# Value products of a key group issued one slot later, in front of that slot's transposes: pooled attention followed by two expert layers

## The chip, the cores and the metric

The kernel runs on one core of a Trainium2 chip. The metric is the device time of one execution in microseconds (us); three runs of the kernel before took 1357.13, 1360.44 and 1360.38 us, a median of 1360.38 us.

## The reference

The input is 4 batches of 8 heads, 1152 tokens, head dimension 64, in float32. Queries are pooled in pairs (the mean of two neighbours), so each head has 576 query rows against 1152 keys:

```
q_pool = q.reshape(B, H, S // 2, 2, D).mean(axis=3)
scores = scale * q_pool @ k.T;  scores -= max
attn = exp(scores) / (sum + 1e-9)
x = attn @ v                      # 4 x 576 rows of 512 columns after joining the heads
h = x @ w_in;  g = max(0.01 * h, h);  x1 = g @ w_out              # 512 -> 2048 -> 512
y = max(x1 @ w1, x1 @ w2, x1 @ w3);  out = y @ w2_out             # 512 -> 768 -> 512
```

## The kernel before

**Attention.** Two heads make a pair: 4 pairs a batch, 16 in all. A pair has two phases, ph 0 (320 query columns a head) and ph 1 (256), and a phase has nine slots, one for each tile of 128 keys. In slot s the program writes the four transposes of p for that key tile (`probs_t`, tile pst, copied by ScalarE, ACT, at line 377 into the buffer pt). Three slots make a key group. In the third slot of a group in ph 0 it also writes three transposes of the "mixed" query tile, one for each key tile of the group (`probs_m`, tile psf, copied by VectorE, DVE, at line 384 into columns 256 to 319 of all three parts of pt). The value products (`values`, tile pv) of a group are six matmuls in the program and twelve records in the trace, from pt and v.

Each slot also carries what `now(s)` has scheduled for it: scores of the next phase (six matmuls into three banks s, or twelve for the mixed tile; DVE takes the maximum at line 334, ACT the exponential at line 335), and the transposes that prepare q and k of the next pair (psq, psk). The same three banks s are used by every score tile from pair 4 on, so a score tile's first matmul waits for the exponential of the tile before.

**Experts.** The experts of a batch run beside the attention of the batch after it. After its own work a slot yields its cost and the caller then issues expert products, in portions that a ratio of costs (RATIO, AHEAD) and a target for each slot (CHAIN less what the slot has issued) set. They are the m products of 512 columns (tile f is the f-th of 16 tiles of the first hidden layer: ACT line 730, DVE line 731 writes the high part of g, GpSimd, POOL, line 732 the remainder), then three products each for y (remainder by POOL, line 670), then the o products of 256 columns. Every operand is split into a high part and a remainder, and a product takes three matmuls for each 128 of depth, the third of which needs the remainder. The event `batch` (after the last value products of a batch) issues what is left of the experts and starts the next; `room` does the same in part.

**What sets the order.** Each engine has one instruction stream. The program order is a priority; a scheduler with a model of durations then fixes the order of every engine, so a change of the program also moves instructions that it does not name. PE (TensorE), DVE, ACT, POOL and the DMA queue of SyncE (SP) then take their own stream in order. Lines 105 to 119 keep the value products of a group together. Line 205 (POOL) adds the two rows of each pair of queries of the next q as soon as the load of line 171 has landed, and that load waits for PE's transposes of the q before it, since there is one buffer. During the experts of batch 0 weights are also decoded: ACT line 589, DVE lines 592 and 595, ACT line 610 and POOL line 611. PSUM: three banks s, one pv, and four banks in rotation for everything else.

Of the kernel before, what the change touches and what calls it, by code (L numbers as in the profile page):

```python
# [22 lines left out]
def kernel(  # L23
# [97 lines left out]
    def transpose(out, in_, eye):  # L121
        return on_pe(nc.tensor.transpose, out, in_, eye)
# [7 lines left out]
    def bank(name):  # L130
        turn[0] += 1
        pool = ps_w["m"] if ps_w and turn[0] % 2 == 0 else ps_m
        return pool.tile([128, 512], F32, tag="m", name=name)
# [30 lines left out]
    def load_pair(n):  # L164
        b, hp = divmod(n, NP)
        h0 = 2 * hp
        qr = raw_p.tile([QP, 2, QC, 2, D], F32, tag="q", name="qraw")
        kr = raw_p.tile([128, 2, KT, D], F32, tag="k", name="kraw")

        def load_q(j0, j1):  # L170
            nc.sync.dma_start(
                out=qr[:, j0:j1].rearrange("p h c r d -> p h (c r) d"),
                in_=q[b, h0 + j0:h0 + j1].rearrange("h (p c) d -> p h c d", p=QP),
            )

        def load_k(j0, j1):
            nc.sync.dma_start(out=kr[:, j0:j1], in_=k[b, h0 + j0:h0 + j1].rearrange("h (p c) d -> p h c d", p=128))

        for j0, j1 in ((0, 1), (1, 2)) if n == 0 else ((0, 2),):
            load_q(j0, j1)  # L180
            load_k(j0, j1)
        raws[n] = [qr, kr]
# [4 lines left out]
    def load_v(n):  # L187
        b, hp = divmod(n, NP)
        h0 = 2 * hp
        if n == 2:  # L190
            t = acc_p.tile([128, KDM, TM], F32, tag="acc", name="vacc").rearrange("p m t -> p (m t)")
            vss[n] = t[:, 0:2 * KT * D].rearrange("p (h c d) -> p h c d", h=2, c=KT)
        elif n == 3:
            t = x_p.tile([128, 2, T], F32R, tag="x", name="vx").bitcast(F32).rearrange("p a t -> p (a t)")
            vss[n] = t.rearrange("p (h c d) -> p h c d", h=2, c=KT)
        else:
            vss[n] = vs_p.tile([128, 2, KT, D], F32, tag="v", name="v")
        nc.sync.dma_start(out=vss[n], in_=v[b, h0:h0 + 2].rearrange("h (p c) d -> p h c d", p=128))

    def pool_q(n, j0=0, j1=2):  # L200
        qr = raws[n][0][:, j0:j1]
        for e in range(2):
            engine = nc.vector if n == 0 and j0 == 0 else nc.gpsimd
            a = [qr[:, :, e::2, r] for r in range(2)]
            engine.tensor_tensor(out=a[1 - e], in0=a[0], in1=a[1], op=ALU.add)

    def prep_k(n, j):
        kr = raws[n][1][:, j].rearrange("p c d -> p (c d)")
        ps = bank("psk")
        for i in range(4):  # L210
            transpose(ps[:, i * 128:(i + 1) * 128], kr[:, i * 128:(i + 1) * 128], ident)
        split_k(n, j, [(slice(e * 512, (e + 1) * 512), ps[64 * e:64 * e + 64, 0:512]) for e in range(2)])
# [75 lines left out]
    def keys_of(p, kt):  # L288
        c, k0 = divmod(kt * 128, SN)
        if c == 2:  # L290
            return p[1][:, k0:k0 + 128]
        return p[0].rearrange("p a b -> p (a b)")[:, kt * 128:(kt + 1) * 128]
# [47 lines left out]
    def normalise(n, ph, i):  # L340
        rs = sums[n, ph]
        c = slice(i, i + 1)
        if n < FREE:
            if i < len(tiles_of(ph)) - 1:
                return
            c = slice(0, i + 1)
        if n < NP:
            nc.vector.tensor_tensor(out=rs[:, c], in0=rs[:, c], in1=rs[:, 8:9 + i], op=ALU.add)
        nc.vector.tensor_scalar(out=rs[:, c], in0=rs[:, c], scalar1=1e-9, scalar2=None, op0=ALU.add)
        nc.vector.reciprocal(out=rs[:, c], in_=rs[:, c])  # L350
        if n >= FREE or i == 4:
            p = ptl[n, ph, i]
            for x in p[2:] or p:
                nc.vector.tensor_scalar(out=x, in0=x, scalar1=rs[:, i:i + 1], scalar2=None, op0=ALU.mult)  # L354
# [13 lines left out]
    def probs_t(n, ph, kt):  # L368
        g = kt % PG
        if g == 0:  # L370
            pts[kt // PG] = pt_p.tile([128, PG, 2 * X0], F32, tag="pt", name="pt")
        w = (X0, T - X0)[ph]
        ps = bank("pst")
        for i in range(4):
            transpose(ps[:, i * 128:(i + 1) * 128], keys_of(ptl[n, ph, i], kt), ident)
        dst = pts[kt // PG][:, g, 0:2 * w].rearrange("p (j c) -> p j c", j=2)[:, :, 0:256]
        nc.scalar.copy(out=dst, in_=ps.rearrange("p (j c) -> p j c", j=2))  # L377
# [65 lines left out]
    def attention():  # L443
        npair = B * NP
        load_pair(0)
        for j in range(2):
            pool_q(0, j, j + 1)
            prep_q(0, j)
            prep_k(0, j)
            if j == 0:  # L450
                for i in range(2):
                    scores(0, 0, i)
                    normalise(0, 0, i)
        load_v(0)
        load_pair(1)
        for n in range(1, NP):
            load_v(n)
        spare_tiles()
        for i in range(2, 5):
            scores(0, 0, i)  # L460
            normalise(0, 0, i)
        phases = [(n, ph) for n in range(npair) for ph in range(2)]
        todo = {}

        def at(slot, cost, f, *args):
            todo.setdefault(slot, []).append((f, args, cost))

        def now(slot):
            spent = 0
            for f, args, cost in todo.pop(slot, []):  # L470
                f(*args)
                spent += cost
            return spent

        for u, (n, ph) in enumerate(phases):
            s0 = u * KT
            if u + 1 < len(phases):
                nxt = phases[u + 1]
                k = len(tiles_of(nxt[1]))
                for i in range(k):  # L480
                    if nxt[0] < NP:
                        t = max(0, s0 + KT - EARLIER - 2 * (k - 1 - i))
                    else:
                        t = s0 + S_AT[nxt[1]][i]
                    at(t, QK * 6 * (1 + (i == 4)), scores, *nxt, i)
                    at(t + 1, 0, normalise, *nxt, i)
            if ph == 0 and n + 1 < npair:
                early = n + 1 < NP
                when = PREP_AT[0 if early else 1]
                at(max(0, s0 + (-8 if early else 1)), 0, pool_q, n + 1)  # L490
                for j in range(2):
                    at(max(0, s0 + when[2 * j]), TR * 3, prep_q, n + 1, j)
                    at(max(0, s0 + when[2 * j + 1]), TR * 4, prep_k, n + 1, j)
                if n + 2 < npair:
                    at(max(0, s0 + (-2 if early else 15)), 0, load_pair, n + 2)
                if n + 1 >= NP:
                    at(s0 + 8, 0, load_v, n + 1)
            if n < FREE:
                at(s0 + 4, TR * 2, spread, n, ph)
        if wide:  # L500
            for c in range(PRE):
                at(6 + c * (2 * NP * KT - 8) // PRE, 0, predecode, c)

        late = []

        def follow():
            pn, pph, pgr = late.pop()
            values(pn, pph, pgr)
            if pgr == KT // PG - 1:
                last = pn % NP == NP - 1  # L510
                if pph == 0 and last:
                    yield "room"
                evac(pn, pph)
                if pph == 1 and last:
                    yield "batch"
            return PG * 4 * (X0, T - X0)[pph] / 2400 + 0.565

        for s in range(len(phases) * KT):
            n, ph = phases[s // KT]
            gr, g = divmod(s % KT, PG)  # L520
            done = 0
            want = CHAIN
            if s == 2 * NP * KT:
                done += yield from follow()
            probs_t(n, ph, gr * PG + g)
            done += TR * 4
            if g == PG - 1 and ph == 0:
                probs_m(n, gr)
                done += TR * PG
                want -= TR * PG  # L530
            c = now(s)
            if g == 0 and late:
                c += yield from follow()
            done += c
            yield done, max(0, want - c)
            yield 0, None
            if g == PG - 1:
                late.append((n, ph, gr))
        yield from follow()
        assert not todo  # L540
# [324 lines left out]
```

## Time and profile before

| | us |
|---|---|
| three runs, median | 1360.38 |
| the profiled execution | 1356.42 |
| its span | 1354.7 |
| PE busy in the span | 1259.0 (93%) |
| PE weight loads | 1015.6 (75%) |
| DVE, ACT busy | 627.9, 633.5 |
| POOL busy | 292.1 |

The span has five stages. Attention of batch 0 runs alone until about 215 us. Stage A (215 to 533 us) is attention of batch 1 beside the experts of batch 0, stage B (533 to 828) and stage C (828 to 1119) the same for the batches after it, and from 1119 us the experts of batch 3 run alone. In the timeline a row's two numbers are its start and the length up to the end of the last instruction merged into it; matmul ends are modelled and overlap the next start, so the time that a row took on PE is read from start to start.

### The profile page before, as it was taken

What the parts mean: (1) busy time and instruction counts of PE and PEld (TensorE: products, weight loads), DVE (VectorE), ACT (ScalarE), POOL (GpSimd) and SP (SyncE); (2) the same over time, 40 slices, a digit from 0 to 9 for tenths busy, and PEclk for the clock granted to TensorE, in tenths of its full rate; (3) what the DMA queues carried; (4) which work ended last, traced back from release to release, by engine and by line L of the source; (5) the groups of instructions that cost most, each with busy time, mean ns of one, the idle gap of its engine ahead of it and who ended that gap; (6) DMA issues with size and microseconds to landing.
All of it is one profiled execution on the core that took longest, in us unless ns stands there. A gap on an engine that the chain in (4) does not pass through costs nothing.

```text
span 1354.7 us, 19162 instructions
## 1 busy us (share of the span) xinstructions
PE 1259.0 (93%) x7376; PEld 1015.6 (75%) x7376; DVE 627.9 (46%) x1106; ACT 633.5 (47%) x1253; POOL 292.1 (22%) x265
## 2 busy tenths in 40 slices
PE   5788878899898989999999989999999999999998
PEld 4556646677676877777787878787877788888888
DVE  5655554556656563455555454545464401222110
ACT  5767665666566664544444344545454422112111
POOL 1111022344454330121121010111110002224110
PEclk8888989999999999999999999999999999999999
DMA  5422053666767663444435344535343244333333
GB/s 158 123 74 57 18 149 118 215 210 209 248 202 229 208 188 131 132 136 131 154 126 157 123 128 163 149 109 150 128 141 116 95 154 154 129 126 124 108 126 109
DMA packets 86902, 193.29 MB, mean 143 GB/s; under 512 B 11292, under 2 KB 41756, under 8 KB 86812
## 3 DMA queue, kind: packets, MB, share of 16 engines
q1 hardware_dynamic: 86812, 192.08, 45.1%
q8 instruction: 58, 0.95, 0.3%
q14 instruction: 32, 0.26, 0.1%
HBM read 146.80 MB, written 35.13 MB: 134 GB/s over the span
## 4 chain that ended last, share of the span: by engine, by line
PE 75%; DMA 9%; DVE 7%; ACT 4%; issue 3%; POOL 2%; DVEq 0%; SPq 0%; ACTq 0%; POOLq 0%
PE m L108 41%; PE pv L108 10%; PE s L108 10%; PE pst L108 6%; PE o L108 6%; DMA wraw<-in_moe_w_out_dram 3%; DMA wraw<-in_moe_w_in_dram 2%; DMA wraw<-in_moe_w_dram 2%; DMA qraw<-in_q_dram 2%; DVE mx L334 1%; DVE wmant L595 1%; DVE mx L324 1%; ACT pt L377 1%; DVE q L259 1%; POOL wsplit L611 1%
## 5 line engine op out<-in xcount | busy, mean ns | idle before, releaser
L108 PE MATMUL m<-x,w 128*128 128x512 f32 x1224 | 308.9, 397 | 0.0
L108 PEld LDWEIGHTS m<-x,w 128*128 128x128 f32 x1224 | 222.7, 188 | 54.0 <-issue 12.8
L377 ACT COPY pt<-pst 128x512 f32<-128x512 f32 x288 | 167.4, 587 | 183.5 <-PE pst L108 182.3
L108 PE MATMUL s<-kt,q 128*128 128x384 f32 x840 | 190.6, 358 | 26.8 <-ACT p L335 14.1
L334 DVE TENSOR_REDUCE mx<-s 128x1 f32<-128x1152 f32 x108 | 146.4, 1355 | 116.2 <-PE s L108 114.9
L108 PEld LDWEIGHTS s<-kt,q 128*128 128x128 f32 x840 | 148.2, 195 | 39.2 <-ACT p L335 16.8
L108 PE MATMUL pst<-ident,p 128*128 128x128 f32 x1080 | 169.4, 277 | 8.4 <-ACT pt L377 3.5
L335 ACT ACTIVATE p<-s,mx 128x1152 f32<-128x1152 f32 x108 | 132.4, 1226 | 83.0 <-DVE mx L334 82.3
L108 PEld LDWEIGHTS pst<-ident,p 128*128 128x128 f32 x1080 | 131.6, 141 | 45.1 <-issue 11.6
L732 POOL TENSOR_TENSOR g<-t,g 128x512 fp32r<-128x512 f32 x64 | 84.5, 1322 | 369.7 <-DVE g L731 355.1
L108 PE MATMUL pv<-pt,v 128*64 128x320 f32 (+1 forms) x1008 | 149.9, 435 | 14.0 <-DVE pt L384 13.4
L108 PE MATMUL m<-g,w 128*128 128x512 f32 x576 | 149.8, 399 | 0.0
L108 PEld LDWEIGHTS m<-g,w 128*128 128x128 f32 x576 | 103.6, 188 | 24.5 <-issue 6.2
L108 PEld LDWEIGHTS pv<-pt,v 128*64 128x64 f32 x1008 | 67.8, 143 | 70.0 <-issue 20.5
L108 PE MATMUL m<-x,wsplit 128*128 128x512 f32 x408 | 108.5, 405 | 1.0 <-DVE kt L223 0.8
L730 ACT ACTIVATE t<-m 128x512 f32<-128x512 f32 x80 | 44.3, 555 | 128.2 <-PE m L108 128.2
L611 POOL TENSOR_TENSOR wsplit<-wmant,wsplit 128x512 fp32r<-128x512 f32 x56 | 74.1, 1327 | 92.8 <-ACT wsplit L610 71.0
L108 PEld LDWEIGHTS m<-x,wsplit 128*128 128x128 f32 x408 | 74.7, 191 | 20.5 <-issue 5.1
L731 DVE CAST g<-t 128x512 fp32r<-128x512 f32 x64 | 28.7, 448 | 111.2 <-ACT t L730 110.7
L760 DVE TENSOR_TENSOR t<-m,t 128x512 f32<-128x512 f32 (+1 forms) x60 | 38.2, 637 | 84.9 <-PE m L108 73.8
L670 POOL TENSOR_TENSOR y<-t,y 128x512 fp32r<-128x512 f32 x24 | 31.7, 1319 | 199.1 <-ACT y L669 199.1
L354 DVE TENSOR_SCALAR p<-p,sums 128x1152 f32<-128x1152 f32 x76 | 66.2, 870 | 2.7
(106 smaller groups left out, 1467.7 us busy)
## 6 DMA issues: line engine op xcount, KB each, us to landing
w<-w SPq DMA_DIRECT2D x168, 512.0 KB, 3.5
w<-wsplit SPq DMA_DIRECT2D x56, 512.0 KB, 5.1
wraw<-in_moe_w_out_dram SPq DMA_DIRECT2D x22, 512.0 KB, 4.1
wraw<-in_moe_w_dram SPq DMA_DIRECT2D x18, 512.0 KB, 4.0
qraw<-in_q_dram SPq DMA_DIRECT2D x15, 576.0 KB
kraw<-in_k_dram SPq DMA_DIRECT2D x15, 576.0 KB, 6.9
q<-q SPq DMA_DIRECT2D x52, 160.0 KB, 4.5
wraw<-in_moe_w_in_dram SPq DMA_DIRECT2D x16, 512.0 KB, 5.7
```

The source lines that it names most:

```text
L108: mm = f(*args, **kwargs)
L259: nc.vector.scalar_tensor_tensor(out=lo, in0=src, scalar=scale, in1=hi, op0=ALU.mult, op1=ALU.subtract)
L334: nc.vector.tensor_reduce(out=mx[:, 0:1], in_=ps[:, :, 0:SN], axis=AX.XY, op=ALU.max, negate=True)
L335: nc.scalar.activation(out=p[2], in_=ps[:, :, 0:SN], func=ACTF.Exp, bias=mx[:, 0:1], accum_out=rs[:, i:i + 1])
L354: nc.vector.tensor_scalar(out=x, in0=x, scalar1=rs[:, i:i + 1], scalar2=None, op0=ALU.mult)
L377: nc.scalar.copy(out=dst, in_=ps.rearrange("p (j c) -> p j c", j=2))
L611: nc.gpsimd.tensor_tensor(out=t[:, 1], in0=r, in1=t[:, 0], op=ALU.subtract)
L670: nc.gpsimd.tensor_tensor(out=t[:, 1], in0=src, in1=t[:, 0], op=ALU.subtract)
L730: nc.scalar.activation(out=t, in_=ps[:, 0:k.n], func=ACTF.Prelu, alpha=0.01)
L731: nc.vector.tensor_copy(out=gt[:, 0], in_=t)
L732: nc.gpsimd.tensor_tensor(out=gt[:, 1], in0=t, in1=gt[:, 0], op=ALU.subtract)
L760: nc.vector.tensor_tensor(out=t, in0=ps[:, 0:k.n], in1=t, op=ALU.max)
```

## The change

Before, the value products of a finished group are written in the first slot of the next group (g == 0), behind that slot's transposes and scheduled work, and then the slot's expert products follow. After, they are written at the start of the second slot (g == 1), in front of its transposes: one portion of expert products, that of the first slot, now stands between. The evacuation of pv and the events `room` and `batch`, which follow the last group of a phase, move with them. The value products' cost now counts in the second slot's portion. The last group of all, and the last group of batch 0, are written where they were.

```
             if s == 2 * NP * KT:
                 done += yield from follow()
+            c = 0
+            if g == 1 and late:
+                c += yield from follow()
             probs_t(n, ph, gr * PG + g)
             done += TR * 4
             if g == PG - 1 and ph == 0:
                 probs_m(n, gr)
...
-            c = now(s)
-            if g == 0 and late:
-                c += yield from follow()
+            c += now(s)
             done += c
```

On PE, at the first key group of pair 8 (start of stage B), before; m are expert products, x the attention output, w the weights:

```order
L108 MATMUL m<-x,w 128x512 x3
L108 MATMUL pst<-ident,p 128x128 x8
L108 MATMUL psf<-ident,p 128x128 x3
L108 MATMUL pv<-pt,v 64x320 x6
L108 MATMUL m<-x,w 128x512 x15
```

And the same group after the change:

```order
L108 MATMUL pst<-ident,p 128x128 x4
L108 MATMUL psf<-ident,p 128x128 x3
L108 MATMUL s<-kt_4345,q_123 128x384
L108 MATMUL s<-kt_4345,q_124 128x384
L108 MATMUL s<-kt_4345,q_123 128x384
L108 MATMUL s<-kt_4345,q_124 128x384
L108 MATMUL s<-kt_4345,q_123 128x384
L108 MATMUL s<-kt_4345,q_124 128x384
L108 MATMUL m<-x,w 128x512 x17
L108 MATMUL pst<-ident,p 128x128 x4
L108 MATMUL m<-x,w 128x512 x7
L108 MATMUL pv<-pt,v 64x320 x6
```

The value products stood directly behind psf; now a tile of scores, 24 m products and four transposes stand between.

On POOL, from the first g of stage B to its last, before (g are the remainders of the 16 expert tiles, qraw the pooling of the next q in two halves):

```order
L732 TENSOR_TENSOR g<-t,g 128x512 x4
L205 TENSOR_TENSOR qraw<-qraw 72x8x64 x2
L732 TENSOR_TENSOR g<-t,g 128x512 x8
L205 TENSOR_TENSOR qraw<-qraw 72x8x64 x2
L732 TENSOR_TENSOR g<-t,g 128x512 x4
```

And after (line numbers below the change are one higher):

```order
L733 TENSOR_TENSOR g<-t,g 128x512 x4
L205 TENSOR_TENSOR qraw<-qraw 72x8x64 x2
L733 TENSOR_TENSOR g<-t,g 128x512 x7
L205 TENSOR_TENSOR qraw<-qraw 72x8x64
L733 TENSOR_TENSOR g<-t,g 128x512
L205 TENSOR_TENSOR qraw<-qraw 72x8x64
L733 TENSOR_TENSOR g<-t,g 128x512 x4
```

The first half of the second qraw has moved in front of the twelfth g, that of tile 11.

On POOL at the end of stage A, before (wsplit is a weight's remainder, mb a copy of row sums, x the attention output):

```order
L611 TENSOR_TENSOR wsplit<-wmant,wsplit 128x512
L360 COPY mb<-sums 128x256
L611 TENSOR_TENSOR wsplit<-wmant,wsplit 128x512 x2
L670 TENSOR_TENSOR y<-t,y 128x512
L205 TENSOR_TENSOR qraw<-qraw 72x8x64 x2
```

And after:

```order
L612 TENSOR_TENSOR wsplit<-wmant,wsplit 128x512 x2
L360 COPY mb<-sums 128x256
L205 TENSOR_TENSOR qraw<-qraw 72x8x64 x2
L612 TENSOR_TENSOR wsplit<-wmant,wsplit 128x512
L671 TENSOR_TENSOR y<-t,y 128x512
```

The last y of batch 0's experts has moved from in front of qraw to behind it and one wsplit.

## Rows read from the trace of the kernel before

**Rows 1.** Busy time by stage: stretch, length, each engine, PEclk, DMA share, GB/s.

```profile
215.00:533.00 318.00, 294.74 (x1687) 233.76 (x1686) 180.00 (x281) 191.05 (x360) 123.93 (x102) 0.98 0.62 201
533.00:828.00 295.00, 284.97 (x1651) 228.29 (x1650) 148.76 (x260) 134.37 (x251) 45.77 (x35) 0.99 0.44 136
828.00:1119.00 291.00, 284.90 (x1675) 228.93 (x1674) 132.88 (x231) 126.25 (x235) 38.99 (x30) 1.00 0.43 135
```

**Rows 2.** Waits of PE, whole span then stage A: total us, times, longest.

```profile
PE pv L108 <- DVE pt L384: 13.4, 15, 3.5
...
PE pv L108 <- DVE pt L384: 6.8, 4, 3.5
PE s L108 <- ACT p L335: 6.6, 5, 4.0
```

**Rows 3.** Timeline of PE, stage A: start, us, what, [idle before, releaser].

```profile
232.25 1.84 PE L108 MATMUL pv<-pt,v 128*64 128x320 f32 x12 [2.33 <-DVE pt L384]
...
369.20 2.29 PE L108 MATMUL s<-kt,q 128*128 128x384 f32 x6 [4.02 <-ACT p L335]
...
478.76 1.83 PE L108 MATMUL pv<-pt,v 128*64 128x320 f32 x12 [3.50 <-DVE pt L384]
```

**Rows 4.** Timeline of PE, stages B and C, four places.

```profile
579.66 0.66 PE L108 MATMUL pst<-ident,p 128*128 128x128 f32 x4 [0.71 <-DVE pt L384]
...
789.77 0.28 PE L108 MATMUL psq<-ident,kraw 128*64 128x128 f32 x1
...
801.20 0.57 PE L108 MATMUL o<-w,y 128*128 128x256 f32 x1 [3.70 <-POOL y L670]
...
834.09 1.31 PE L108 MATMUL s<-kt,q 128*128 128x384 f32 x6 [1.45 <-ACT p L335]
```

**Rows 5.** Busy time and PEclk behind two waits, columns as in rows 1.

```profile
478.70:481.00 2.30, 2.23 (x14) 1.20 (x15) 0.44 (x2) 1.45 (x3) 0.00 (x0) 1.00 0.34 127
...
801.20:804.90 3.70, 3.70 (x13) 1.50 (x13) 0.00 (x0) 0.37 (x1) 0.00 (x0) 0.54 0.14 40
```

**Rows 6.** Timeline of SP and POOL in stage B: loads of q and their pooling.

```profile
572.72 0.33 SPq L171 DMA_DIRECT2D qraw<-in_q_dram  x1
...
580.63 2.52 POOL L205 TENSOR_TENSOR qraw<-qraw 72x512 f32<-72x512 f32 x2 [17.59 <-DMA qraw<-in_q_dram]
...
645.68 0.33 SPq L171 DMA_DIRECT2D qraw<-in_q_dram  x1
...
652.11 2.50 POOL L205 TENSOR_TENSOR qraw<-qraw 72x512 f32<-72x512 f32 x2 [6.28 <-DMA qraw<-in_q_dram]
...
717.72 0.33 SPq L171 DMA_DIRECT2D qraw<-in_q_dram  x1
...
723.21 2.50 POOL L205 TENSOR_TENSOR qraw<-qraw 72x512 f32<-72x512 f32 x2 [1.09 <-PE pst L108]
...
799.38 1.77 POOL L670 TENSOR_TENSOR y<-t,y 128x512 fp32r<-128x512 f32 x1
```

**Rows 7.** The page's costliest groups: busy, mean ns of one, idle before.

```profile
L611 POOL TENSOR_TENSOR wsplit<-wmant,wsplit 128x512 fp32r<-128x512 f32 x56 | 74.1, 1327 | 92.8 <-ACT wsplit L610 71.0
```

**Rows 8.** Timeline of PE in stage B, for durations from start to start.

```profile
542.29 3.70 PE L108 MATMUL m<-x,w 128*128 128x512 f32 x15
545.84 0.60 PE L108 MATMUL pst<-ident,p 128*128 128x128 f32 x4
546.19 3.02 PE L108 MATMUL m<-x,w 128*128 128x512 f32 x12
549.04 1.23 PE L108 MATMUL s<-kt,q 128*128 128x384 f32 x6
550.11 0.86 PE L108 MATMUL m<-x,w 128*128 128x512 f32 x3
...
566.43 0.60 PE L108 MATMUL psk<-ident,kraw 128*128 128x128 f32 x4
566.96 1.84 PE L108 MATMUL pv<-pt,v 128*64 128x320 f32 x12
```

More of the change, by code (lines that the diff above doesn't have):

```diff
@@ L524, in attention @@
                 done += yield from follow()
+            c = 0
+            if g == 1 and late:
+                c += yield from follow()
             probs_t(n, ph, gr * PG + g)
@@ L530, in attention @@
                 want -= TR * PG
-            c = now(s)
-            if g == 0 and late:
-                c += yield from follow()
+            c += now(s)
             done += c
```

## The prediction

> **What bounds the kernel now.** I read the busy time by stage first, then the waits of TensorE (PE) in each stage, then the timeline at every one of them. In the stage table [rows 1] stage A (attention of batch 1 beside the experts of batch 0, with weights still being decoded) has PE busy for 294.74 of 318 us, and stages B and C (batches 2 and 3) 284.97 of 295 and 284.90 of 291. PE bounds all of them, and what the change can win is PE's idle time: 23.3 + 10.0 + 6.1 = 39.4 us. Moving instructions takes no work off PE. The table of waits [rows 2] says whom PE waited for: 13.4 us (15 times, 6.8 us of it in stage A) are value products (pv) waiting for DVE's line 384; none of these waits lies in batch 0. That is the copy of the transposed mixed tile psf, which writes columns 256 to 319 of all three key tiles of the group; so even the first of the value products needs it.
>
> Two more things have to be seen. An engine takes its instructions in order: the o product stood still for 3.70 us for y, which POOL could not make while it was held by line 205, the pooling of the next q, itself waiting for a DMA [rows 4, 6]. And a long wait costs more than itself: after that one the granted clock was 0.54 for 3.7 us (between the levels of 1.2 and 2.4 GHz), 3.7 x 0.46 = 1.7 us; after a wait of 3.50 us at 478.76 it stayed at 1.00 [rows 3, 5]. Of the seven waits of 2.3 us and more in stages A and B five were followed by such a fall, so I charge 1.7 us for each wait above 3 us.
>
> **The change part by part.** In batch 0 nothing stands between the two places, so PE's order is the same until the first expert products. In stages A to C, 72 groups of value products move behind one more portion of expert products.
>
> *What goes (1).* Before, psf stands directly in front of pv at most of the 15 places; the first piece of order shows one. After the change, adding up what PE has between psf and pv, I find 2.7 us or more for nearly all groups. An m product takes (545.84 - 542.29) / 15 = 0.237 us, four transposes 0.35, six score products 1.07, four transposes of k 0.53 [rows 8]. The copy needed up to 0.9 us in stages B and C, so its waits go. Two exceptions: the first group of stage A keeps only three m products, 0.7 us, of the 2.33 us that pv waited there [rows 3], so 1.6 us stay; and one group in each of B and C keeps four transposes between psf and pv, where it was the transposes that waited (0.71 us at 579.66 [rows 4]), as they will again. Gain 13.4 - 1.6 = 11.8 us.
>
> *What goes (2).* The wait of 3.70 us for y: in the new order of stage B some 12.5 us of PE's work stand between the last transposes of q and the o product that needs y, against 7.3 us before, and the chain from the transposes at 789.77 to the product at 801.20 took 11.4 us [rows 4]. It goes with its slow clock: 3.70 + 1.7 = 5.4 us.
>
> *What goes (3).* At the start of stage C scores waited 1.45 us for the exponential of the tile before [rows 4]; 18 o products instead of 9 now stand between, about 1.1 us more. Gain 1.1 us.
>
> *What goes (4).* Scores of stage A waited 6.6 us for exponentials, five times [rows 2], because DVE stood at a decode step in front of the maximum. Of 31 gaps between score tiles there, 10 had 4.6 us of PE's work or less; now 5 have. I take half: 3.2 us. The bounds are all of it with one slow clock (8.3) and, since other decode steps may now stand in front of a maximum, a loss of two stalls like that of 369.20 [rows 3], 2 x (4.02 + 1.7) = 11.4.
>
> *What comes (1).* The third piece of order shows POOL in stage B: the first half of line 205 now stands in front of the remainder g of expert tile 11, where both halves stood behind it. The same holds in stage C. The load of q starts when PE has transposed the last of the q before: 645.68, landing at 652.11, 6.43 us [rows 6]; elsewhere 5.49 to 7.91. From the transposes: 0.2 to the issue, 6.4 to land, 1.25 for half of line 205, 1.3 for the subtraction (line 611's 1.33, the same size [rows 7]), 9.2 us until g is there. The product that needs it (the 12th of the first m of the third group) is reached earlier: 3 m, 2 scores, 9 m, 4 scores, psf, 4 transposes, 4 of k and 2 m, that is 14 x 0.237 + 1.07 + 0.26 + 0.35 + 0.53 = 5.5 us, 5.6 with the issue. PE then waits 9.2 - 5.6 = 3.6 us and loses 1.7 of clock: 5.3 us, twice, 10.6 us. Behind the waiting product stand PE's transposes and scores, so nothing else covers it. Bounds: 2.7 each with the shortest landing and no fall of the clock, 6.8 with the longest.
>
> *What comes (2).* At the end of stage A the last y now stands behind line 205 and a weight's subtraction on POOL, as y of stage B did behind line 205. From the transposes of q: 0.2 + 6.4 + 2.5 + 1.3 + 1.77 = 12.2 us [rows 6, 7]. PE's work to the product that needs it: 12 m (2.84), six scores (1.07), psf 0.26, transposes 0.35 and 0.53, and 17 o products of half an m each (2.0), 7.1 us. Wait 5.1, with the clock 6.8 us; bounds 4.2 and 8.3.
>
> On the load's time the page DMA: Bandwidth & Descriptors of the Trainium skill (section Anatomy of one DMA) gives a fit, about 2.0 us plus the bytes at 436 GB/s; for 576 KB that is an estimate of 3.4 us against the 6.43 measured. By the page the three new waits would be 0.6, 0.6 and 2.1 us and the sum -18.2. No load of q in these rows came near it, with the weight loads beside it, so the measurement stands.
>
> Costed at nothing: the two pt buffers (a group's products now come two slots before its buffer is refilled), the one pv bank (three slots between the last and the first group, as before), the start of the next batch's experts (nine products that don't need the last x stand first), and the tail of experts alone after 1119 us, whose order is unchanged.
>
> **Sum.** -11.8 - 5.4 - 1.1 - 3.2 + 6.8 + 10.6 = -4.1 us. The profiled execution took 1356.42 us (1354.7 of it the span), which gives 1352.3; it lies 4.0 us below the median of the three runs, 1360.38, against which I predict: 1356.3. What can be told from no change is about 0.3%, 4.1 us.
>
> **Rivals.**
> *POOL's detour is cheap*, chance 0.26. The load of q lands in 5.5 us, as at 717.72 [rows 6], and waits under 3 us bring no fall of the clock: the new waits are 2 x 2.7 + 4.2 = 9.6 us and the sum -21.5 + 9.6 = -11.9, 1348.5 us. For it: two loads of weights ran beside the longest landing, and one wait of 3.50 us left the clock alone. Against it: four of the six landings that I read lay between 6.4 and 7.0 us. The page's 3.4 us would push this to 1342.2; I give that 0.03 of the 0.26.
>
> *Stage A's decode takes over*, the slower side, chance 0.22. DVE stands at line 592 or 595 for a weight or for POOL while a maximum is queued behind it, as before 369.20. It decides from the first stall of that size: -4.1 + 3.2 + 5.7 = +4.8, 1365.2 us; with two, 1370.9. For it: 6.6 + 6.8 us of stage A's idle time came this way, and the order of decode steps against maxima is reshuffled there. Against it: score gaps have grown.
>
> *The copy still holds PE*, chance 0.08: the change moves pv, but the transposes that now follow closely need psf's bank and wait instead, as at 579.66. Then the 13.4 - 6.8 = 6.6 us of stages B and C come back: +2.5, 1362.9 us.
>
> **How the numbers follow.** My forecast, the sum as it stands, has 0.44 and by itself a range of 1350 to 1363; it is split 0.20 faster, 0.23 no difference, 0.01 slower. With the first rival faster, the second slower and the third no difference: faster 0.46, same 0.31, slower 0.23. The range over all reaches from below the first rival to above the one-stall case of the second: 1344 to 1369.
>
> **What would show it.** In the changed profile: pv waiting for DVE's line 384 for about 2 us in all instead of 13.4; one m product in each of stages B and C waiting 3 to 4 us for POOL's g, with line 205 before it on POOL and the granted clock near 0.55 behind it; one o product near the end of stage A waiting about 5 us for POOL's y; none of that kind at the end of stage B. I am wrong if the m products don't wait for g (then POOL was free in time, the first rival), or if stage A has grown while B and C have not (the second).

## The result

The changed kernel took 1345.55 us, the median of four runs (1336.52 to 1350.29), against 1359.69 us for four runs of the kernel before (1357.13 to 1360.44): a ratio of 0.9891, with an interval of 0.9861 to 0.992. It is 14.1 us faster; the forecast was 4.1 us, 1356.3 us against 1360.38. The time lies inside the range of 1344 to 1369 us, near its lower end and nearest to the rival called "POOL's detour is cheap" (1348.5 us). A later comparison gave 1345.29 us, ratio 0.991 (0.9884 to 0.9937).

The profiled execution of the changed kernel is one of its slowest, 1350.29 us with a span of 1348.5 us, so it shows only 6.1 us of the gain. Its stages, cut within 0.1 us of the first expert product of each batch's experts, stand in the first fence, those of the kernel before at the same events in the second (columns as in [rows 1]):

```profile
220.60:543.60 323.00, 299.90 (x1697) 237.30 (x1696) 189.80 (x288) 192.15 (x363) 124.91 (x101) 0.96 0.62 201
543.60:831.20 287.60, 283.95 (x1669) 227.89 (x1668) 149.05 (x258) 133.81 (x251) 46.30 (x35) 1.00 0.46 140
831.20:1109.40 278.20, 274.63 (x1603) 218.37 (x1602) 128.78 (x226) 122.54 (x227) 39.53 (x30) 1.00 0.43 133
```

```profile
218.58:542.29 323.71, 297.77 (x1693) 235.82 (x1691) 182.18 (x285) 193.09 (x362) 122.64 (x101) 0.97 0.62 201
542.29:836.78 294.49, 285.69 (x1670) 229.74 (x1668) 148.75 (x260) 133.92 (x252) 45.77 (x35) 0.99 0.45 138
836.78:1115.65 278.87, 274.23 (x1607) 219.91 (x1605) 129.05 (x227) 122.73 (x227) 38.99 (x30) 1.00 0.42 131
```

The gain sits in stage B: -6.9 us, against -0.7 in A and -0.7 in C. Batch 0, whose order on PE the change leaves alone, took 2 us longer in this execution; that is scatter, since nine profiles with this same order there (those of both kernels, e2, e9 and e10) have it at 215.6 to 222.1 us. Stage A has less idle time on PE (323.00 - 299.90 = 23.1 us against 25.9) but a granted clock of 0.96 instead of 0.97, which eats most of it.

Of the waits of PE over the whole span of the changed kernel, these bear on the prediction (columns as in [rows 2]; after the change L384 is still the copy of psf, L671 and L733 are the remainders of y and g, and L731 and L743 the two lines that stood at 730 and 742; the dots stand for rows left out):

```profile
PE s L108 <- ACT p L335: 8.7, 4, 2.9
...
PE pv L108 <- DVE pt L384: 3.6, 3, 2.1
PE psk L108 <- ACT acc L743: 3.5, 1, 3.5
PE m L108 <- POOL g L733: 3.4, 4, 1.5
PE o L108 <- POOL y L671: 3.1, 1, 3.1
...
PE m L108 <- ACT t L731: 2.4, 1, 2.4
```

The 13.4 us for the copy [rows 2] have become 3.6. Neither the 3.70 us for y at the end of stage B nor the 1.45 us for an exponential behind it [rows 4] has a successor. The new waits that the prediction named are there: one o product for y, and the m products for g.

What is left of the copy's waits are the exceptions that the prediction named (timeline of PE, two of the three places):

```profile
235.77 1.88 PE L108 MATMUL pv<-pt,v 128*64 128x320 f32 x10 [2.10 <-DVE pt L384]
...
579.09 0.66 PE L108 MATMUL pst<-ident,p 128*128 128x128 f32 x4
580.49 1.83 PE L108 MATMUL pv<-pt,v 128*64 128x320 f32 x12 [0.74 <-DVE pt L384]
```

The first group of stage A waits 2.10 us instead of 2.33 [rows 3]. The group of stage B in which four transposes alone stand between psf and pv now waits at pv, 0.74 us, where the transposes had waited 0.71 [rows 4]; stage C has one like it.

The three new waits on PE, the first two with the row before them:

```profile
500.40 2.15 PE L108 MATMUL o<-wsplit,y 128*128 128x256 f32 x16
505.67 0.50 PE L108 MATMUL o<-wsplit,y 128*128 128x256 f32 x2 [3.12 <-POOL y L671]
...
648.23 2.13 PE L108 MATMUL m<-g,w 128*128 128x512 f32 x8
651.58 0.50 PE L108 MATMUL m<-g,w 128*128 128x512 f32 x1 [1.22 <-POOL g L733]
...
939.36 0.50 PE L108 MATMUL m<-g,w 128*128 128x512 f32 x1 [1.50 <-POOL g L733]
```

And what POOL did in front of the first two:

```profile
500.13 2.53 POOL L205 TENSOR_TENSOR qraw<-qraw 72x512 f32<-72x512 f32 x2 [6.58 <-DMA qraw<-in_q_dram]
502.62 1.26 POOL L612 TENSOR_TENSOR wsplit<-wmant,wsplit 128x512 fp32r<-128x512 f32 x1
503.84 1.77 POOL L671 TENSOR_TENSOR y<-t,y 128x512 fp32r<-128x512 f32 x1
...
649.01 1.29 POOL L205 TENSOR_TENSOR qraw<-qraw 72x512 f32<-72x512 f32 x1 [6.75 <-DMA qraw<-in_q_dram]
650.27 1.26 POOL L733 TENSOR_TENSOR g<-t,g 128x512 fp32r<-128x512 f32 x1
```

The mechanism is the one foretold: line 205 stands idle for its load, then the remainder, then PE goes on at once. The lengths are not: 3.12 us for y where I had 5.1, and 1.22 and 1.50 us for g where I had 3.6. The clock behind the three (busy time and PEclk, columns as in [rows 1]):

```profile
505.60:509.60 4.00, 3.93 (x16) 1.85 (x17) 0.37 (x1) 0.65 (x2) 0.02 (x1) 0.62 0.30 107
651.50:655.50 4.00, 3.92 (x22) 2.44 (x23) 2.23 (x5) 1.01 (x2) 1.27 (x2) 1.00 0.82 249
939.30:943.30 4.00, 3.94 (x23) 2.49 (x24) 2.23 (x5) 1.01 (x2) 1.24 (x2) 1.00 0.87 268
```

It fell behind the wait of 3.12 us, to a mean of 0.62 over 4 us (4.00 x 0.38 = 1.5 us lost), and not behind the two of 1.22 and 1.50 us.

### The profile page after: what moved, and what is told of

Same layout as the page of the kernel before. It is cut to its first block, busy times and chain, and to the rows that moved or that the text cites. A ratio compares the mean times of both kernels' runs of the same rounds, so it can differ in the third digit from the quotient of the medians.

```text
span 1348.5 us, 19140 instructions
## 1 busy us (share of the span) xinstructions
PE 1261.8 (94%) x7376; PEld 1016.0 (75%) x7376; DVE 637.0 (47%) x1106; ACT 632.5 (47%) x1253; POOL 295.5 (22%) x265
## 4 chain that ended last, share of the span: by engine, by line
PE 75%; DMA 9%; DVE 8%; ACT 5%; issue 2%; POOL 1%; DVEq 0%; SPq 0%; ACTq 0%; POOLq 0%
PE m L108 39%; PE pv L108 11%; PE s L108 10%; PE pst L108 7%; PE o L108 5%; DMA wraw<-in_moe_w_out_dram 3%; DMA wraw<-in_moe_w_dram 2%; DMA qraw<-in_q_dram 2%; DVE q L259 1%; DMA wraw<-in_moe_w_in_dram 1%; ACT q L255 1%; DVE wmant L596 1%; DVE mx L324 1%; ACT pt L377 1%; DVE mx L334 1%
## 5 line engine op out<-in xcount | busy, mean ns | idle before, releaser
L108 PE MATMUL pst<-ident,p 128*128 128x128 f32 x1080 | 174.0, 282 | 10.7 <-ACT pt L377 3.8
L108 PEld LDWEIGHTS pst<-ident,p 128*128 128x128 f32 x1080 | 128.1, 142 | 67.2 <-issue 35.4
L108 PEld LDWEIGHTS s<-kt,q 128*128 128x128 f32 x840 | 151.5, 197 | 33.4 <-ACT p L335 10.2
L733 POOL TENSOR_TENSOR g<-t,g 128x512 fp32r<-128x512 f32 x64 | 84.1, 1315 | 355.3 <-DVE g L732 340.8
L731 ACT ACTIVATE t<-m 128x512 f32<-128x512 f32 x80 | 44.2, 554 | 105.4 <-PE m L108 104.7
L671 POOL TENSOR_TENSOR y<-t,y 128x512 fp32r<-128x512 f32 x24 | 32.2, 1343 | 181.6 <-ACT y L670 181.5
L354 DVE TENSOR_SCALAR p<-p,sums 128x1152 f32<-128x1152 f32 x76 | 69.9, 919 | 2.5
```

The lines of the kernel that those rows point to most:

```text
L108: mm = f(*args, **kwargs)
L671: nc.gpsimd.tensor_tensor(out=t[:, 1], in0=src, in1=t[:, 0], op=ALU.subtract)
L731: nc.scalar.activation(out=t, in_=ps[:, 0:k.n], func=ACTF.Prelu, alpha=0.01)
L733: nc.gpsimd.tensor_tensor(out=gt[:, 1], in0=t, in1=gt[:, 0], op=ALU.subtract)
```

## The experiments

Each ratio is against the kernel before in the same comparison, with its 95% interval; "span less clock" means the span times the mean granted clock of a run. Where stages are compared, they are cut in every profile at the first expert product of each batch.

**e1, e8, e11: the changed kernel again.** No edit; e8 and e11 are single profiles.

> The changed kernel once more, unaltered, to find its spread: its four runs lie between 1336.5 and 1350.3 us with granted clocks from 0.986 to 0.975, those of before between 1357.1 and 1360.4. Theory 1 (the gain is PE's waits for line 384's copy, 13.4 to 3.6 us, the rest is scatter of the clock): 1346 us, 8 to 15 us under before. Theory 2 (the reordering as a whole lowers the number of long waits and so the falls of the clock): 1343 or less, with runs near 1336 as often as near 1350.

> The changed kernel once more, for one more profile. If the place where its runs differ (1336.5 to 1352.0 us) is the attention of batch 0 and stage A, where the two profiles so far and e2's differ by 4 to 7 us, then B, C and the tail are 287.5, 270.5 and 247 us again and only the first 545 us differ. If the spread is a matter of the clock throughout, all stages differ in proportion.

> The changed kernel once more, for the place of its scatter: 1340 to 1350 us, with the clock lower in some 20 us stretches of batch 0 and stage A than in the other profiles and the same in stages B and C.

Measured: e1 1345.29 us (1340.28 to 1352.0), ratio 0.991 (0.9884 to 0.9937), close to theory 1's 1346; e8 1347.26, e11 1345.28 us. Over the four profiles the wait for y was 3.1, 2.7, 2.0 and 2.3 us and the longest for g 1.1 to 1.7. Stage A took 323.0, 322.6, 321.3 and 319.2 us, B 287.0 to 287.6 in all four, C 277.6 to 279.0: most of the scatter between profiles is stage A's, as far as four can tell. The granted clock was 0.90 or 0.91 in batch 0, 0.96 or 0.97 in stage A and 1.00 in B and C in each of the four, so e11's expectation of a lower clock in its batch 0 and stage A did not come true.

**e12: the kernel before again.** No edit.

> The kernel before once more: 1354 to 1361 us, the waits for the copy of line 384 13 us as in the first profile, the differences to it in the stretches of batch 0 and stage A with a lower clock.

Measured: 1360.0 us. The waits for the copy are 13.3 us again; but the y of stage B is later, and stage B takes 297.0 us instead of 294.5, which the expectation had not foreseen. First PE, then POOL and SP in this profile:

```profile
804.21 0.58 PE L108 MATMUL o<-w,y 128*128 128x256 f32 x1 [5.83 <-POOL y L670]
```

```profile
800.39 2.54 POOL L205 TENSOR_TENSOR qraw<-qraw 72x512 f32<-72x512 f32 x2 [17.45 <-DMA qraw<-in_q_dram]
```

```profile
790.90 0.33 SPq L171 DMA_DIRECT2D qraw<-in_q_dram  x1
```

The load took 800.39 - 790.90 = 9.5 us here, and PE waited 5.83 us where it had waited 3.70 [rows 4].

**e10: the y of stage B set free, nothing else.** In the kernel before, both halves of line 205 for pair 13 are kept behind the last y of stage B; PE's order is unchanged. The lines that note each remainder in `rests` are left out here.

```
+    HELD = {13: (1, 'y', 5)}
-            engine.tensor_tensor(out=a[1 - e], in0=a[0], in1=a[1], op=ALU.add)
+            add = engine.tensor_tensor(out=a[1 - e], in0=a[0], in1=a[1], op=ALU.add)
+            if n in HELD:
+                tc.add_manual_dep(add.ins, rests[HELD[n]], NOSYNC, ...)
```

> The kernel before with both halves of line 205 for pair 13 behind the last y of stage B; TensorE's order is unchanged. It isolates one term of the forecast, the wait of 3.70 us for y that the change also removed. Theory 1 (the wait and the clock behind it): 5.4 us under before. Theory 2 (the wait alone): 3.7 us under. Rival (the wait hid another one: the scores of stage C or the value products wait in its place): no difference.

Measured: 1350.09 us, ratio 0.9954 (0.9932 to 0.9975), 6.2 us. The same o product, PE:

```profile
797.38 0.60 PE L108 MATMUL pst<-ident,p 128*128 128x128 f32 x4
797.73 0.36 PE L108 MATMUL o<-w,y 128*128 128x256 f32 x1
798.02 1.84 PE L108 MATMUL pv<-pt,v 128*64 128x320 f32 x12
```

No wait, and the twelve value products behind it take 1.8 us, not the 3.2 that they took from 801.70 to 804.91 in the kernel before. Stage B (columns as in [rows 1]) is the one that became shorter:

```profile
542.87:831.67 288.80, 283.70 (x1670) 229.20 (x1669) 147.64 (x260) 133.82 (x252) 46.06 (x35) 1.00 0.45 141
```

That is 5.7 us less than the 294.49 before, and no other stage differs by more than 0.6 us. The wait of 3.70 us and the 1.7 us of clock behind it make 5.4 us: theory 1, this term pays its wait and its clock. The interval of the ratio alone is too wide to exclude the wait alone. Of the 6.9 us by which the change shortens stage B in its profile, this one wait is worth 5.7.

**e3: the copy early, the value products where they were.**

```
-            if g == PG - 1 and ph == 0:
+            if g == PG - 2 and ph == 0:
                 probs_m(n, gr)
```

> The kernel before, value products where they were, but the mixed tile's transposes and its copy written in the second slot of a key group instead of the third, so that the copy is not in front of the value products. Theory 1 (the copy of line 384 is what the change wins back): pv's waits for line 384 fall from 13.4 us to under 3, and the time by 8 to 13 us, to about 1348, although no value product is moved. Theory 2 (the place of the value products among scores and expert products matters, not the copy): the waits go but the time stays within 4 us of before, 1356 to 1364.

Measured: 1345.3 us, ratio 0.9911 (0.9888 to 0.9934). Its waits:

```profile
PE pst L108 <- DVE kt L223: 14.0, 14, 3.9
...
PE s L108 <- ACT p L335: 9.5, 6, 2.9
...
PE o L108 <- POOL y L670: 1.1, 1, 1.1
```

No pv waits for line 384 any more, and the kernel is as fast as the changed one without a value product moved. That does not show that the copy's waits are what the change wins, because transposes of p now wait 14.0 us for line 223, the split of k, where pv had waited 13.4 us for the copy. The stages A, B and C, and one row of the waits in stage C alone:

```profile
221.63:533.32 311.69, 293.57 (x1693) 233.17 (x1691) 183.12 (x285) 191.30 (x361) 123.16 (x101) 0.98 0.65 209
533.32:823.89 290.57, 284.75 (x1670) 229.01 (x1668) 147.68 (x261) 135.15 (x252) 44.91 (x35) 1.00 0.45 140
823.89:1102.89 279.00, 275.01 (x1606) 219.80 (x1605) 127.81 (x227) 122.99 (x227) 39.15 (x30) 1.00 0.42 131
```

```profile
PE pst L108 <- DVE kt L223: 3.0, 5, 1.2
```

Stage C is no shorter than before (278.87 us): the copy's 3.6 us there went and 3.0 us for line 223 came. Stage B is 3.9 us shorter, where the wait for y shrank to 1.1 us, and stage A 12.0 us, where 6.8 us for the copy went and 7.5 for line 223 came, but four other waits shrank too (for lines 335, 758, 742 and 731, 10.8 us in sum; all of PE's waits in the stage fell by 7.7 us and its clock rose from 0.97 to 0.98). So e3 is as fast as the change by another way: its gain sits in stage A, that of the change in stage B. Over the whole span PE waited 79.0 us, 12.3 less than before.

**e4: one slot later, but behind the slot's work.**

```
-            if g == 0 and late:
+            if g == 1 and late:
                 c += yield from follow()
```

> One part of the change: the value products one slot later, but behind that slot's transposes and scheduled work instead of in front. Theory 1: the copy is covered even better (the least work between psf and pv is 1.8 us against 0.4), so the time is that of the changed kernel or 2 us less, 1343 to 1348. Rival (the place in front of the transposes matters, since it separates the transposes of two slots and gives ACT time to copy them): 4 us and more above the changed kernel, with more waits of transposes for ACT's line 377.

Measured: 1377.13 us, ratio 1.0142 (1.0121 to 1.0164), 19 us slower than before. Scores wait for exponentials 16 times:

```profile
PE s L108 <- ACT p L335: 19.6, 16, 3.0
```

One of the places in stage B:

```profile
609.70 1.31 PE L108 MATMUL s<-kt,q 128*128 128x384 f32 x6
610.85 1.55 PE L108 MATMUL m<-x,w 128*128 128x512 f32 x6
612.24 0.60 PE L108 MATMUL pst<-ident,p 128*128 128x128 f32 x4
614.35 2.35 PE L108 MATMUL s<-kt,q 128*128 128x384 f32 x12 [1.51 <-ACT p L335]
616.63 1.51 PE L108 MATMUL pv<-pt,v 128*64 128x256 f32 x12
```

The value products stand behind the mixed score tile; in the kernel before they stand in front of it, and with the expert products that are there too, 8.0 us lie between the starts of the two score tiles (600.84 to 608.88), against 4.65 here with the wait. The rival named another wait, of transposes for line 377; it came as well, 7.3 us beside the experts, where the kernel before has none. All of PE's waits grew by 10.6 us (101.9 against 91.3), about half of the loss; the other half no row that I read explains, and it stays open.

**e5: in front of the transposes, but in the first slot.**

```
-            if g == 1 and late:
+            if g == 0 and late:
                 c += yield from follow()
```

> The value products stand in front of a slot's transposes, as in the changed kernel, but in the first slot of the next group (g == 0) and not one slot later. Between psf and pv there are now 1.07 us of work or less in half of the groups of stages A to C (0 at least, 0.53 in several), against 2.8 us and more after the change. Theory 1 (the change pays through the time it gives the copy of line 384, nothing else): the copy's waits in stages B and C fall from 6.6 us to about 2, those of stage A only from 6.8 to about 5; with some of stage A's score waits gone the time is 1351 to 1355 us, between before (1357.8 in the last comparison) and after (1345.3). Theory 2 (the place in front pays by itself, since it spreads the scores: no gap between two score tiles below 1.5 us, against 16 such gaps before and 6 after): as fast as after or faster, 1346 us or less. Rival: the value products in front stand in the way of the next transposes and so of everything that ACT does: slower than before, 1362 us or more.

Measured: 1359.99 us, ratio 1.0017 (0.9995 to 1.0038): no difference, and none of the three expectations. The trace shows two effects that cancel. Stages A to C take 886.9 us against 897.1 before; the waits for the copy there are 5.0 us, not 13.4. The wait for y at the end of stage B is still there (4.4 us), so these 10.2 us owe nothing to it. Stage C is the cleanest: the waits of pv for the copy in it before, then in e5, and stage C of e5:

```profile
PE pv L108 <- DVE pt L384: 3.6, 6, 0.9
```

```profile
PE pv L108 <- DVE pt L384: 1.1, 2, 0.7
```

```profile
842.93:1119.68 276.75, 274.56 (x1613) 219.67 (x1612) 129.32 (x230) 123.54 (x230) 39.53 (x30) 1.00 0.43 133
```

It is 2.1 us shorter than the 278.87 before, and all of PE's waits in it fell by 2.5 us; three profiles with the old order there (both of the kernel before, and e10) agree within 0.1 us. Here the copy's waits pay about their length. But batch 0 takes 232.8 us against 218.6, where PE, in that stretch alone, now waits:

```profile
PE s L108 <- ACT p L327: 14.9, 11, 2.9
PE psq L108 <- ACT pt L377: 7.1, 4, 2.9
PE s L108 <- ACT p L335: 6.5, 3, 2.9
```

(12.0, 2.2 and 3.4 us in the same rows of the kernel before.) Theory 1 was thought out for the stages with experts and holds there; I had overlooked that this edit, unlike the change, also alters PE's order in batch 0, where there are no expert products to fill the gap. Beside experts the place in front is enough; the second slot is what spares batch 0.

**e2 and e9: POOL's detour taken out of the changed kernel.** The edit of e10, with

```
+    HELD = {9: (0, 'y', 5), 11: (1, 'g', 11), 15: (2, 'g', 11)}
```

> The changed kernel, with line 205's pooling for pairs 9, 11 and 15 kept behind the last y of batch 0 and the g of expert tile 11 of batches 1 and 2 on POOL; PE's order is the same. Theory 1 (waits of an in-order PE add up): the waits of 3.12, 1.22 and 1.50 us for POOL go, the time falls 4 to 8 us under the changed kernel, to about 1340. Rival (what waits there is covered, or the pooling comes too late and PE's transposes of q wait instead): within 3 us of the changed kernel, with a new wait of psq for line 205.

> The changed kernel with both halves of line 205 for pairs 9, 11 and 15 behind the last y of batch 0's experts and the twelfth g of stages B and C (e2_pool_behind had moved only one half, and only at the y: the twelfth g still had one half in front). TensorE's order differs from the changed kernel's at three places. Theory 1 (POOL's detour costs what the trace shows): the waits of 2.0 to 3.1 us for y and of 1.1 to 1.5 us twice for g go, 5 us in all: 1340 us, as e2 or a little under. Rival (e2 was 4 us under the changed kernel by scatter, since it took only 1.8 us of the wait for y and left the waits for g): no more than 3 us under the changed kernel's 1345, 1342 to 1344.

Measured: e2 1341.45 us, ratio 0.9879 (0.9857 to 0.9901); e9 1338.09 us, ratio 0.9869 (0.9842 to 0.9897). In e2 the edit bound one of the two halves of line 205 only, and moved one only at the y of stage A: the waits for g (2.6 us in sum) were still there. e9 moves both halves. Its waits for g are

```profile
PE m L108 <- POOL g L737: 1.5, 4, 0.4
```

against 3.4 us, and the o product waits no more. Stage C, 277.6 to 279.0 us in the four profiles of the changed kernel, is 276.81 us here:

```profile
820.42:1097.23 276.81, 274.40 (x1603) 218.25 (x1602) 128.36 (x226) 122.24 (x227) 39.50 (x30) 1.00 0.42 133
```

By the ratios e9 is 3 to 6 us under the changed kernel (0.9891 and 0.991 against 0.9869); by the mean spans (1336.8 of six runs, 1343.5 of twelve) 6.7 us, which is too much, since the kernel before was also 2 to 4 us faster in e9's comparison (1355.9 against 1357.82 and 1359.69). The intervals overlap, so the size of the detour is known only so far; that it costs 17.4 us, as forecast, is excluded.

**e7: e3 with one half of line 205 for pair 13 behind the last y of stage B.**

> e3_before_early_copy with line 205 for pair 13 kept behind the last y of stage B; the value products where they were before, the order on TensorE the same as in e3. Theory 1 (a wait for POOL costs its own length): the 1.07 us wait of the o product for y at the end of stage B goes, 1 us under e3's 1345.3, 1344. Rival (it costs its clock too): 2.5 to 3 us under, 1342.5.

Measured: 1344.81 us, ratio 0.9889 (0.9865 to 0.9913). The wait for y is gone; against e3 (0.9911) the difference is too small for these intervals to tell the two expectations apart.

**e6: both, the changed kernel with the early copy of e3 and the edit of e2.**

> The changed kernel, with the transposes of the mixed tile and their copy one slot earlier (as in e3_before_early_copy) and line 205 for pairs 9, 11 and 15 kept behind the remainders (as in e2_pool_behind). Between psf and pv there are 5.7 us of work or more in all groups beside experts. Theory 1 (what still waited for the copy in the changed kernel, 2.10 us in stage A and twice 0.74, is all that the earlier copy can give): about 2.5 to 3.5 us under e2_pool_behind (1341.5), 1338 to 1339. Rival: the gains don't add, since the mixed scores come directly behind other score tiles again (20 gaps under 1.5 us, against 6 in the changed kernel) and wait for the exponential: 1341 to 1345.

Measured: 1339.39 us, ratio 0.9846 (0.9821 to 0.9871), better than both kernels. No pv waits for the copy; its longest rows in stages A to C are

```profile
PE s L108 <- ACT p L339: 8.7, 6, 2.7
PE m L108 <- DVE acc L750: 3.2, 3, 1.1
```

It lies 2.1 us under e2's median, and its ratio 0.3% under e2's: theory 1's direction, not separable from no gain by the runs. In the profiles its stages B and C are 3.2 and 2.9 us shorter than e2's, but batch 0 and stage A 5.4 and 1.6 us longer. e6 with both halves bound, as in e9, wasn't tried.

## Why the prediction came out on the right side, and where its sizes failed

**PE bounds, and what the change wins is PE's idle time: right.** All of PE's waits fell from 91.3 us to 82.4 in the profile. Over the runs (43 of the kernel before, 12 of the changed one) the span less clock fell from 1323.3 to 1314.9 us, 8.4 us. The same two differences, waits and span less clock, are -4.9 and -5.2 in e10, -12.3 and -10.6 in e3, -16.1 and -14.9 in e6, -11.4 and -11.3 in e7, -1.1 and -2.1 in e5; in e2 (-14.3, -9.6) and e9 (-16.3, -12.4) the waits overstate it by 4 to 5 us, and e4 is the exception named above.

**What goes (1), the copy, -11.8: the waits nearly right, their worth shown in part.** 13.4 - 3.6 = 9.8 us of waits went. The first group of stage A kept 2.10 us where the forecast had 1.6, and the two groups costed at nothing kept 0.74 us each. That such a wait pays about its length is shown in stage C of e5; in stage A of the changed kernel other waits moved with it, and no run takes them apart.

**What goes (2), the y of stage B, -5.4: right, and the best shown.** Gone; it is worth 6.2 us alone in e10, and 5.7 us of stage B in its profile. The second profile of before shows that it could be longer than the row I used.

**What goes (3), the score of stage C, -1.1: right.** The 1.45 us are gone.

**What goes (4), scores in stage A, -3.2: right in size, by a guess.** The forecast took half of the waits for want of anything better. The waits for line 335 from 218.5 us to the start of stage B fell from 9.2 us to 5.7 (5.3 to 7.4 over the four profiles). But other waits came in stage A that no term held: 3.5 us for an attention output's accumulation (L743, 2.3 before) and 2.4 for L731, while one of 3.0 us for line 758 went.

**What comes (1), the twelfth g, +10.6: the step that failed most.** Measured 0.36 + 1.22 + 0.36 + 1.50 = 3.4 us, no clock. The mechanism stood; three numbers under it were off. The products of PE up to the wait were miscounted: I took the m products behind psk as 2 and then the waiting one, because the merged rows of the order hide which operand each needs. With buffer numbers the rows say (g_5738 is the late remainder's tile):

```
L108 MATMUL psk_5806<-ident_120,kraw_5394 128x128 x4
L108 MATMUL m_5788<-g_5738,w_5633 128x512 x2
L108 MATMUL m_5844<-g_5592,w_5697 128x512 x3
L108 MATMUL m_5844<-g_5635,w_5697 128x512 x3
L108 MATMUL m_5788<-g_5738,w_5633 128x512
```

The scheduler had put six products of the next tile in front of the one that waits, 6 x 0.237 = 1.4 us of cover. The load took 649.01 - 643.38 = 5.6 us until line 205 began, not 6.4. And no fall of the clock followed. Had I carried the six products, 3.6 - 1.4 = 2.2 us would have been the term, without clock.

**What comes (2), the y of stage A, +6.8: too large in the same way.** 3.12 us and 1.5 of clock, 4.6. The late step of the first o product stands behind the whole group of 18 and 16 of the next, so 34 half-size products, not 17, lay in front, and with four more transposes PE had 9.8 us of work from the transposes of q to its wait, not 7.1 (492.78 to 502.55); the load was slower than I took, 500.13 - 492.98 = 7.15 us. Such loads now took 5.6, 7.15 and 9.5 us. By the fit that the Trainium skill gives (DMA: Bandwidth & Descriptors, section Anatomy of one DMA, there for GpSimd's own DMA path, while this load is issued by SyncE) the estimate is 3.4 us; no run here came near, so the measurements decided rightly. With these two terms as measured (3.4 and 4.6 us instead of 10.6 and 6.8) the sum would have been -13.5 us, near the 14.1 and 12.5 us measured; that it comes so near is luck in part, since all of PE's waits fell by 8.9 us only.

**The clock: the charge for g was wrong, the rest is open.** The prediction charged 1.7 us for each long wait and so 1.7 x 3 - 1.7 = 3.4 us more for the change. The two waits for g, charged with 3.4 us, were followed by no fall. Over the runs the mean granted clock was 0.9788 after and 0.9759 before; span x (1 - clock) is 28.6 us (standard error 1.3) against 32.6 (0.5), 4.0 us less. By this measure the change won 8.4 us in span less clock, where my terms without clock came to 7.5, and 4.0 us in clock, where they came to a loss of 3.4. So of the 8.4 us that the mean gain of the runs (12.5 us of span) exceeds the forecast of 4.1 by, 7.4 are booked as clock: 3.4 of them the charge for g, and 4.0 without a known cause. The measure is rough: it also counts the clock that is granted while PE stands idle (batch 0 alone, 218.6 us at 0.91, makes about 20 us of it), and the four profiles of the changed kernel, three of them among its slower runs, have 29.6 to 33.7 us by it, no less than the 29.8 and 34.0 of the two profiles of before. So no trace shows where the faster runs save it. That the copy's waits had cost clock is not shown either: behind its wait of 3.50 us the clock stayed at 1.00 [rows 5].

**The rivals.** "POOL's detour is cheap" was nearest. Its conditions held in stage B, the load in 5.6 us (it said 5.5) and no fall of the clock behind the waits for g, and not in stage A (7.15 us, and 1.5 us of clock); that its number came near is luck in part, since the waits were shorter than its 2.7 and 4.2 us by products in front that it had not counted either. Its 5.5 us is the time until line 205 began, and there it was PE that released line 205 [rows 6], so the load may have landed sooner. Stage A's decode taking over: stage A is not longer in any profile. The copy still holding PE through the transposes: 0.74 us twice.

**Open.** Why runs of the same kernel spread over 1336.5 to 1352.0 us after the change, more widely than the 1343.67 to 1346.1 of e3's four (batch 0 alone, in one order, scatters by 6.5 us over nine profiles); what the change wins in stage A; and what the second half of e4's loss is.

## What to carry to other kernels

Look for a transfer of one engine's result that another needs a moment later, and give it work to stand behind, by moving either end. Then look at what waits in its place: in stage C of e5 hardly anything did and the stage became 2.1 us shorter, in stage C of e3 another wait of the same length did and it stayed as long. Compare stage by stage before two kernels of equal time are given one cause: e3 won in stage A what the change won in stage B. When a step is moved, follow what it pushes on the engines that are not the bound. Here a pooling that waits for a load held one remainder before, and freeing that one alone gave 6.2 us (e10); after the change it stood in front of three others, and taking it back out (e9) gave some more. And before a new wait is priced, name the very instruction that needs the late operand, since a scheduler puts others in front of it.

## What the runs showed of the hardware that was not expected

Loads of q of one size took 5.6 to 9.5 us from their issue until line 205 began, and the same place in the same program 6.9 us (790.01 to 796.93) in one execution and 9.5 in another; with it the wait of one o product went from 3.70 to 5.83 us. The mean granted clock of one and the same program differs from run to run, 0.971 to 0.982 in the kernel before, and 0.001 of it is 1.4 us of the span. Batch 0 took 215.6 to 222.1 us in nine profiles with one and the same order on PE. A fall followed a wait of 3.12 us here and did not follow one of 3.50 us in the kernel before [rows 3, 5].
